# Moving a bias load on ScalarE's queue and a row copy on SyncE's queue in a fused attention and feed-forward kernel

## The chip, the cores and the metric

The kernel runs on one core of a Trainium2 chip. The metric is the device time of one execution in microseconds (us). A core has five engines that run their own instruction streams: TensorE (PE, matrix products; its weight loads are shown as PEld), VectorE (DVE), ScalarE (ACT), GpSimd (POOL) and SyncE (SP), which here only issues transfers. ScalarE and GpSimd issue transfers too. SPq, ACTq and POOLq are the instruction queues of these engines, and each works in order. Transfers of all queues share 16 DMA engines.

## What is computed

x has 2048 rows of 640 values. Its normalised rows xn go through two branches that are added to x:

```python
xn = _layernorm(x, axis=-1)
return x + _A_ref(xn, A_wqkv, A_wo) + _B_ref(xn, B_w1, B_b1, B_w2, B_b2)

# A: 32 heads of 20 values; each row looks at 8 rows, 2 apart, itself the first
q, k, v = (xn @ wqkv)            # three 640-wide parts
logits = einsum("bhsd,bhswd->bhsw", q, kg) * scale
o = einsum("bhsw,bhswd->bhsd", softmax(masked logits), vg)
A = o @ wo
# B: 640 -> 1536 -> 640
B = gelu(xn @ w1 + b1) @ w2 + b2
```

The code above is the reference cut to its core; kg and vg are the keys and values gathered at the 8 rows.

## The kernel before

The 2048 rows are worked on in four chunks of 512 rows, and a chunk in four blocks of 128. A chunk's stages are: statistics of its rows, normalised rows xn, their transposition into xnT (640 values on partitions), the projections to q, k and v, the products q times shifted k on VectorE (piece `qk`, L436), their folding (`pa`, L471), the logits as a matmul with head_of (`lg`, L479), softmax, the weighted values, the output product with wo, and the first and second feed-forward products (`f1`, L595, with gelu on ScalarE, `ge`, L611, and `o`, L631 and L633).

The order of the work is written out by hand. Each small step is a named piece, and the list `ORDER` (L42) says in which order the pieces are emitted. Every engine then runs its own instructions in that order, and an instruction waits on semaphores for what it needs. So moving a name in `ORDER` moves its instructions in the stream of each engine that the piece uses, and nothing else. In a name such as `xn12` the first digit is the chunk and the second the block.

Before `ORDER` starts, the loads are issued (L136 to L149): on SyncE x's block 0, wq, wk, blocks 2 and 3 of chunk 0, wv, chunk 1's rows and w1; on ScalarE x's block 1 (L138) and the bias b1 (L139). b1 comes as 12 rows of 128 values into the tile `b1_rt`, whose 16 rows GpSimd has set to zero (L124). The piece `tb` (L459) transposes it on TensorE into a PSUM tile, and the piece `b1` (L462) copies that on VectorE to `b1T`, from where each gelu takes its bias. The first gelu is `ge0_0`. `ldx` loads chunks 2 and 3 of x, `ldo` loads wo and b2, and `ld2` loads w2, all on SyncE.

Chunk 0 is normalised on VectorE (L268), transposed on TensorE (`tp`, L283) and copied to xnT by VectorE and ScalarE (`tc`, L288). Its projections are made by halves of 256 rows: `hj` is a group of matmuls (L383), and `hc` is ScalarE's copy of the result (L398). The first digit of these names is 0, 1 or 2 for q, k and v, the second is the half, and the third a group of columns, where group 2 is one 128-wide tile and the others are two. `hj102`, `hj101` and `hj100` are thus the keys of the first half.

Chunk 1's rows are normalised on ScalarE (L266: `xn13`, `xn10`, `xn11`, `xn12` in this order) and transposed by transposing DMAs on SyncE (`tc13`, `tc10`, `tc11`, `tc12`, L295). Chunk 1's first projection is `pj101` (L339); it needs all four blocks. ScalarE also makes the row sums of chunk 2 in between (`su`, L224, and `sq`, L231).

The output is put together in device memory: `xp0`, `xp1` and `xp2` copy rows of x to the output (L304, on SyncE), later accumulating DMAs on GpSimd add b2 (`xb`, L308) and the product of each block (`od`, L644). `xp0` copies chunk 0's 512 rows, 640 KB.

The PSUM tiles of projections, logits, first feed-forward products and `tb` come from one pool of six buffers (psA).

Of the kernel before, what the change touches and what calls it, by code (L numbers as in the profile page):

```python
# [17 lines left out]
P = 128  # L18
DH = D // H
PAD = (W - 1) * DIL  # L20
KT, FT = D // P, F // P
# [19 lines left out]

ORDER = """  # L42
wb st00a sum1 wa pad01 st00 rs00 ldx rc00 xn00a tp00a xn00b tp00b tc00a ga neg1 sq1 rs01 rc01 tc00b gb2 mean1 xn01
tp01 gb3 gb4 tc01a gd tc01b ho ge gc1 st03a st03 rs03 gc0 hj102 rc03 hc102 tb b1 hj101 hc101 st02a st02 rs02 hj100
hc100 xn03 tp03 tc03 pk hj202 rc02 xn02 tp02 tc02 gc4 hj201 hc201 hj111 st11a st10a hc111 st12a hj012 hc012 st11 hc202
st13a st13 hj112 hc112 st10 st12 rs1 qk010 rc1 qk000 qk011 hj110 f10_0 ge0_0 hj212 xn13 qk001 xn10 tc13 xn11 hc212
pa010 hj011 hj010 hc010 f10_11 f10_2 hc110 hc011 qk031 qk021 ge0_11 f10_10 xp0 qk020 pa000 su23 f10_6 xn12 ge0_10
qk030 pa020 su21 tc10 tc11 su22 hj200 hc200 f10_3 ge0_3 pa030 pa011 f10_9 tc12 su20 ng2 sq21 ge0_9 pa021 pj101 pc101
ge0_2 sq23 pj111 pj102 pj114 pc114 xp2 pc102 pj110 pc110 pj104 pa001 ge0_6 pa031 lg0 pc111 cl0 ldo xb3 xb2 pc104 mask
m0 mx0 ex0 pj112 pj103 pc103 pj113 pc113 ss0 ri0 pad11 pj100 pc100 pc112 qk121 qk120 hj211 sq20 hc211 qk101 ld2 pj124  # L50
qk100 sq22 pc124 f10_4 rs2 f11_6 pj121 rc2 ge0_4 pa120 qk110 f11_2 f10_1 ge0_1 pa121 qk111 xn21 pj123 pc123 ge1_6
# [26 lines left out]
def kernel(  # L78
# [16 lines left out]
    nc = tc.nc  # L95
# [27 lines left out]
    b1_rt = consts.tile([MW, P], BF16, name="b1_rt")  # L123
# [6 lines left out]
    def load_x(b0, b1):  # L130
        nc.sync.dma_start(x_sb[:, b0:b1, :], x_nb[:, b0:b1, :])  # L131
# [4 lines left out]
    load_x(0, 1)  # L136
    nc.vector.memset(x_sb[:, 1, 0:16], 0.0)
    nc.scalar.dma_start(x_sb[:, 1, :], x_nb[:, 1, :])  # L138
    nc.scalar.dma_start(b1_rt[0:FT, :], B_b1.rearrange("(t p) -> t p", p=P))  # L139
    for a in range(1):  # L140
        ks = slice(a * KT // 1, (a + 1) * KT // 1)
        nc.sync.dma_start(wqkv[0][:, ks, :], wqkv_v[:, ks, 0:D])
# [8 lines left out]

    def do_ldx():
        load_x(2 * BPC, NCH * BPC)

    def do_ld2():
        w2_v = B_w2.rearrange("(t p) n -> p t n", p=P)
        for c in range(2):
            ts = slice(c * FT // 2, (c + 1) * FT // 2)
            nc.sync.dma_start(w2_sb[:, ts, :], w2_v[:, ts, :])
# [20 lines left out]
    mask = consts.tile([H, W, MW], BF16, name="mask")  # L180
# [489 lines left out]
    def piece(name, fn, *args):  # L670
        assert name not in pieces
        pieces[name] = lambda: fn(*args)

    for name in "tb b1 mean1 ho ldx ld2 ldo xl oclo ohi ochi ochd mask pk".split():
        piece(name, locals()[f"do_{name}"])
    for u, a, b, eng, own in (("a", 0, 2, "ve", "lo"), ("b", 2, KT, "se", "hi")):
        piece(f"xn00{u}", do_xn, 0, 0, a, b)
# [119 lines left out]
```

## Time and profile before

| | |
|---|---|
| median of 3 runs | 207.31 us (206.66 to 207.37) |
| the profiled execution's own time | 207.25 us |
| its span, first to last instruction | 205.3 us |
| mean granted TensorE clock | 1.000 |
| packets moved by DMA | 27335, 31.77 MB, mean 155 GB/s |

The span is what the trace covers; the profiled execution's own time is 1.95 us longer. All times of single instructions are counted from the span's start. A row of the timeline gives start, duration, engine, line of the kernel, operation, output and input with shapes, the number of instructions merged into the row, and in brackets how long the engine stood idle before it and what ended that. A row of a list of DMA issues ends with the size and the median time from issue to landing. Busy times by stretch give for each engine the busy time and, in brackets, the number of instructions, then the granted clock, the DMA engines' mean busy share and the rate in GB/s.

### The profile page before, as it was taken

The page shows a single profiled execution, that of the slowest core. Times are in us where ns is not written, and L with a number is a line of the kernel's source. Part 1 is how long each engine was busy: PE and PEld are TensorE (multiplying, and loading weights), DVE is VectorE, ACT ScalarE, POOL GpSimd, SP SyncE. Part 2 cuts the span into 40 slices and gives each one's busy share as a digit, 9 for nine tenths or more (in the row PEclk, how much of TensorE's full clock was granted, in tenths as well). Part 3 has the DMA queues.
Part 4 walks back from the last instruction along what each step waited for, and adds up shares of the span by engine and source line. Part 5 has one row for each costly group of instructions (what it writes and reads, how often), then busy time and mean ns, then how long its engine had stood idle before and what let it go on. Part 6 is the DMA issues. An engine that isn't in the chain of part 4 may idle for free.

```text
span 205.3 us, 3230 instructions
## 1 busy us (share of the span) xinstructions
PE 200.1 (97%) x1261; PEld 111.1 (54%) x1261; DVE 181.6 (88%) x226; ACT 127.1 (62%) x246; POOL 34.6 (17%) x49
## 2 busy tenths in 40 slices
PE   8899999999999999999999999999999999999994
PEld 3798655464454555554555555445544455555552
DVE  3489999389998999769999999899998999699992
ACT  6388998999966998856425735564535794111210
POOL 2000000440000242202260060003104223111120
PEclk9999999999999999999999999999999999999999
DMA  6999599899259299989999067005462997972253
GB/s 209 390 395 374 185 140 323 303 258 199 58 100 252 86 173 190 156 128 182 189 188 191 8 73 122 0 0 68 103 134 32 164 190 118 209 116 28 28 66 64
DMA packets 27335, 31.77 MB, mean 155 GB/s; under 512 B 9272, under 2 KB 22072, under 8 KB 27320
## 3 DMA queue, kind: packets, MB, share of 16 engines
q0 software_dynamic: 7408, 12.78, 39.0%
q1 hardware_dynamic: 19600, 18.58, 32.8%
q8 instruction: 10, 0.16, 0.3%
q10 hardware_dynamic: 312, 0.20, 0.3%
q14 instruction: 5, 0.04, 0.1%
HBM read 10.00 MB, written 7.54 MB: 85 GB/s over the span
## 4 chain that ended last, share of the span: by engine, by line
PE 90%; DMA 4%; ACT 3%; issue 1%; SPq 0%; DVE 0%
PE lo L631 29%; PE pps L339 24%; PE hps L595 22%; PE hi L633 7%; PE gps L383 5%; DMA wq_sb<-in_A_wqkv_dram 3%; DMA xnT<-xn 2%; ACT xn L266 2%; PE gps L352 1%; PE L L479 1%; ACT qT L398 1%; PE tp L283 0%; ACT trash L224 0%; ACT hT L611 0%; SPq L131 0%
## 5 line engine op out<-in xcount | busy, mean ns | idle before, releaser
L595 PE MATMUL hps<-xnT,w_sb 128*128 128x512 bf16 x240 | 55.6, 379 | 0.0
L436 DVE TENSOR_TENSOR half<-qT,kT 128x2560 bf16<-128x2560 bf16 x32 | 46.7, 1484 | 1.0 <-PE L L479 0.9
L631 PE MATMUL lo<-w_sb,hT 128*128 128x512 bf16 x144 | 41.3, 379 | 0.0
L595 PEld LDWEIGHTS <-w_sb 128*128 128x128 bf16 x240 | 23.1, 98 | 26.2
L471 DVE TENSOR_TENSOR half<-half 128x1024 bf16<-128x1024 bf16 (+1 forms) x44 | 36.5, 881 | 0.0
L638 ACT CAST osb<-lo 128x512 bf16<-128x512 f32 x15 | 8.8, 584 | 37.1 <-PE hi L633 18.3
L633 PE MATMUL hi<-w_sb,hT 128*128 128x128 bf16 x144 | 31.5, 219 | 0.0
L611 ACT ACTIVATE hT<-hps,b1T 128x512 bf16<-128x512 f32 x36 | 24.0, 692 | 6.5 <-PE hps L595 5.6
L563 DVE TENSOR_TENSOR half<-vT,x_sb 128x2560 bf16<-128x2560 bf16 x16 | 23.0, 1487 | 3.3 <-DMA x_sb<-e 3.2
L644 POOL DMA_DIRECT2D out_dram<-osb x15 | 13.7, 959 | 72.2 <-ACT osb L639 72.2
L573 POOL DMA_DIRECT2D half<-half x12 | 15.6, 1302 | 56.0 <-DVE half L563 56.0
L563 DVE TENSOR_TENSOR half<-vT,ax 128x2560 bf16<-128x2560 bf16 x16 | 23.0, 1482 | 1.2 <-PE L L479 1.2
L631 PEld LDWEIGHTS <-hT 128*128 128x128 bf16 x144 | 14.1, 98 | 17.2 <-issue 0.4
L631 PE MATMUL lo<-wo,oT 128*128 128x512 bf16 x80 | 23.1, 379 | 0.0
L339 PE MATMUL pps<-xnT,wq_sb 128*128 128x512 bf16 x75 | 18.5, 380 | 0.4 <-DMA xnT<-xn 0.4
L339 PE MATMUL pps<-xnT,wv_sb 128*128 128x512 bf16 x75 | 18.3, 379 | 0.0
L339 PE MATMUL pps<-xnT,wk_sb 128*128 128x512 bf16 x75 | 18.0, 379 | 0.0
L633 PE MATMUL hi<-wo,oT 128*128 128x128 bf16 x80 | 16.9, 219 | 0.0
L176 ACT ACT_TABLE_LOAD x12 | 15.4, 1283 | 0.9 <-PEq L781 0.7
L633 PEld LDWEIGHTS <-hT 128*128 128x128 bf16 x144 | 14.1, 98 | 1.9
L582 DVE TENSOR_TENSOR half<-half 128x1280 bf16<-128x1280 bf16 x16 | 13.1, 821 | 0.5 <-DMA half<-half 0.4
L403 ACT CAST vT<-pps 128x512 bf16<-128x512 f32 x15 | 8.8, 587 | 6.9 <-PE pps L339 6.9
(91 smaller groups left out, 262.3 us busy)
## 6 DMA issues: line engine op xcount, KB each, us to landing
half<-half POOLq DMA_DIRECT2D x12, 640.0 KB, 6.9
w_sb<-in_B_w_dram SPq DMA_DIRECT2D x4, 960.0 KB, 11.3
out_dram<-osb POOLq DMA_DIRECT2D x15, 160.0 KB, 3.5
ax<-e SPq DMA_DIRECT2D x8, 256.0 KB, 4.7
x_sb<-e SPq DMA_DIRECT2D x8, 256.0 KB, 4.9
out_dram<-b2bc POOLq DMA_DIRECT2D x3, 640.0 KB, 9.6
x_sb<-in_A_x_dram SPq DMA_DIRECT2D x1, 1280.0 KB, 12.9
out_dram<-x_sb SPq DMA_DIRECT2D x2, 640.0 KB, 4.7
```

What stands on the lines that cost most here:

```text
L176: nc.scalar.activation(warm[:], nc.const_aps.tensor(0.0, [P, 1], F32), func)
L339: nc.tensor.matmul(ps[:], lhsT=wqkv_p[which][:, ti, to, :], rhs=xnT[:, ti, :], start=(ti == 0), stop=(ti == KT - 1),)
L436: nc.vector.tensor_tensor(out=half[:, j, h], in0=q[:, :, at].unsqueeze(1).to_broadcast([P, W // 2, KT, P]), in1=window(k, h, at), op=ALU.mult,
L471: nc.vector.tensor_tensor(out=kept, in0=kept, in1=gone, op=ALU.add)
L563: nc.vector.tensor_tensor(out=half[:, j, h], in0=window(qkv_tile(n, 2), h, cs), in1=ax_view(n)[:, j, ws, :].unsqueeze(2).to_broadcast([P, ...
L573: nc.gpsimd.dma_start(a, b, accum_op=ALU.add, max_dma_last_dim=CUT)
L582: nc.vector.tensor_tensor(out=a, in0=a, in1=b, op=ALU.add)
L595: nc.tensor.matmul(ps[:], lhsT=w1_sb[:, ti, ft * P : (ft + 1) * P], rhs=tiles["xnT", n][:, ti, :], start=(ti == 0), stop=(ti == KT - 1),)
L611: nc.scalar.activation(hT, tiles["hps", n, ft][:], ACT.Gelu_apprx_tanh, bias=b1T[:, ft : ft + 1], scale=1.0)
L631: nc.tensor.matmul(lo[:], lhsT=lhs, rhs=rhs[:, 0:CH], start=first, stop=last)
L633: nc.tensor.matmul(hi[:, 0 : D - CH], lhsT=lhs, rhs=rhs[:, CH:D], start=first, stop=last)
L644: nc.gpsimd.dma_start(rows, tiles["osb", n, bl][:], accum_op=ALU.add)
```

## The change

Two pieces of work change their place.

The load of b1 leaves the head of the kernel, where it stood second in ScalarE's queue, and becomes a piece of its own, `ldb`, between `hc102` and `hj101`. The pieces `tb` and `b1`, which stood there, go behind `st12`, the last of chunk 1's statistics, ahead of `rs1` and `qk010`.

The piece `xp0` leaves its place between `tc13` and `tc10` in SyncE's queue and goes behind `tc12`, ahead of `xp2`.

```diff
-hc102 tb b1 hj101 ... hj112 hc112 st10 st12 rs1 qk010
+hc102 ldb hj101 ... hj112 hc112 st10 st12 tb b1 rs1 qk010

-f10_10 xp0 qk020 ... tc10 tc11 ... tc12 su20
+f10_10 qk020 ... tc10 tc11 ... tc12 xp0 su20

     nc.scalar.dma_start(x_sb[:, 1, :], x_nb[:, 1, :])
-    nc.scalar.dma_start(b1_rt[0:FT, :], B_b1.rearrange("(t p) -> t p", p=P))

+    def do_ldb():
+        nc.scalar.dma_start(b1_rt[0:FT, :], B_b1.rearrange("(t p) -> t p", p=P))

-    for name in "tb b1 mean1 ho ldx ld2 ldo ...
+    for name in "tb b1 mean1 ho ldx ldb ld2 ldo ...
```

The first two parts are lines of `ORDER`, cut to the names around the moved ones. No instruction is added or taken away.

More of the change, by code (lines that the diff above doesn't have):

```diff
@@ L43 @@
 wb st00a sum1 wa pad01 st00 rs00 ldx rc00 xn00a tp00a xn00b tp00b tc00a ga neg1 sq1 rs01 rc01 tc00b gb2 mean1 xn01
[L44 to L48, printed above, removed]
+tp01 gb3 gb4 tc01a gd tc01b ho ge gc1 st03a st03 rs03 gc0 hj102 rc03 hc102 ldb hj101 hc101 st02a st02 rs02 hj100 hc100
+xn03 tp03 tc03 pk hj202 rc02 xn02 tp02 tc02 gc4 hj201 hc201 hj111 st11a st10a hc111 st12a hj012 hc012 st11 hc202 st13a
+st13 hj112 hc112 st10 st12 tb b1 rs1 qk010 rc1 qk000 qk011 hj110 f10_0 ge0_0 hj212 xn13 qk001 xn10 tc13 xn11 hc212
+pa010 hj011 hj010 hc010 f10_11 f10_2 hc110 hc011 qk031 qk021 ge0_11 f10_10 qk020 pa000 su23 f10_6 xn12 ge0_10 qk030
+pa020 su21 tc10 tc11 su22 hj200 hc200 f10_3 ge0_3 pa030 pa011 f10_9 tc12 xp0 su20 ng2 sq21 ge0_9 pa021 pj101 pc101
 ge0_2 sq23 pj111 pj102 pj114 pc114 xp2 pc102 pj110 pc110 pj104 pa001 ge0_6 pa031 lg0 pc111 cl0 ldo xb3 xb2 pc104 mask
@@ L672, in piece @@
         pieces[name] = lambda: fn(*args)
-    for name in "tb b1 mean1 ho ldx ld2 ldo xl oclo ohi ochi ochd mask pk".split():
+    for name in "tb b1 mean1 ho ldx ldb ld2 ldo xl oclo ohi ochi ochd mask pk".split():
         piece(name, locals()[f"do_{name}"])
```

## The prediction

> **What bounds the kernel now.** I read the page's first parts and then one narrow view at a time. The page says which engine carries the end:
>
> ```profile
> span 205.3 us, 3230 instructions
> PE 200.1 (97%) x1261; PEld 111.1 (54%) x1261; DVE 181.6 (88%) x226; ACT 127.1 (62%) x246; POOL 34.6 (17%) x49
> ```
>
> TensorE (PE) is busy for 200.1 of 205.3 us. An edit can therefore pay only by filling one of PE's few gaps, or cost by making a new one. The busy time by stretch shows where the gaps are (behind the stretch: its length, then PE's busy time; the granted clock is the figure before the last two):
>
> ```profile
> 6.77:29.85 23.08, 23.08 (x206) 18.47 (x206) 20.00 (x37) 19.03 (x40) 0.00 (x0) 1.00 0.95 291
> 29.85:30.28 0.43, 0.00 (x1) 0.03 (x1) 0.43 (x2) 0.43 (x2) 0.00 (x0) 1.00 0.44 167
> 30.28:202.00 171.72, 171.72 (x1028) 90.33 (x1029) 157.65 (x178) 103.45 (x197) 33.26 (x32) 1.00 0.70 134
> ```
>
> From the first weights' arrival at 6.77 until 202 us PE has one gap, 0.43 us long, before 30.28. The clock is 1.00 throughout, so no throttling enters the sum. The chain that ended last, in order of time (start, duration), says what that gap waits for:
>
> ```profile
> 25.73 0.81 ACT xn L266
> 26.56 3.58 DMA xnT<-xn
> 30.28 6.64 PE pps L339 x30
> ```
>
> Chunk 1's first projection needs all four transposed blocks. ScalarE (ACT) finishes the last one, xn12, at 26.54 (25.73 + 0.81); its transposing DMA is issued at 26.56 and has landed 3.58 us later, at 30.14. PE's only inner gap hangs on the very DMAs that the second edit reorders.
>
> **Second edit: the copy xp0 goes behind the transposes.** SyncE's queue (SPq) around them, from the timeline, then the landing times of the transposes issued at 23.11, 24.88 and 26.56:
>
> ```profile
> 21.12 1.32 SPq L295 DMA_TRANSPOSE xnT<-xn  x1
> 22.55 0.50 SPq L304 DMA_DIRECT2D out_dram<-x_sb  x1
> 23.11 1.68 SPq L295 DMA_TRANSPOSE xnT<-xn  x1
> 24.88 1.23 SPq L295 DMA_TRANSPOSE xnT<-xn  x1
> 26.56 2.34 SPq L295 DMA_TRANSPOSE xnT<-xn  x1
> 28.99 0.53 SPq L304 DMA_DIRECT2D out_dram<-x_sb  x1
> ...
> xnT<-xn SPq DMA_TRANSPOSE x1, 5.8
> xnT<-xn SPq DMA_TRANSPOSE x1, 4.6
> xnT<-xn SPq DMA_TRANSPOSE x1, 3.6
> ```
>
> Chunk 2's four transposes follow each other with no copy between them; they are the undisturbed case (first the four issues, then their median time to landing):
>
> ```profile
> 53.65 5.23 SPq L295 DMA_TRANSPOSE xnT<-xn  x4
> xnT<-xn SPq DMA_TRANSPOSE x4, 2.4
> ```
>
> There a transpose lands in 2.4 us. Behind xp0 they take 5.8, 4.6 and 3.6, and the last issue stretches to 2.34 us: the 640 KB copy stands ahead in the same queue, and the backlog drains one transpose at a time. With xp0 out of its place the second can be issued at about 22.55 and the third at 23.9 (an issue of 1.3 later), so both are down by 26.3 (23.9 + 2.4). The last still starts at 26.56, since ACT sets that, and after 2.4 us lands at 28.96. PE arrives at 29.85, so the DMA is 0.9 us early and the gap goes: **-0.43 us**. More isn't there, since PE is busy on both sides of it. The condition is a landing below 3.29 us (29.85 - 26.56).
>
> What is late next? The first matmul behind the gap that needs VectorE (DVE) is lg0, and the last DVE group before it is this:
>
> ```profile
> 31.21 4.76 DVE L471 TENSOR_TENSOR half<-half 128x2048 bf16<-128x2048 bf16 x6
> 36.86 1.05 PE L479 MATMUL L<-half,head_of 128*32 128x512 bf16 x16
> ```
>
> DVE ends at 35.97; PE will ask at 36.43 instead of 36.86, so 0.46 us of cover is left. Past lg0, DVE's softmax starts from ACT's copy of lg0's result and moves with it. On SPq the last transpose's issue falls from 2.34 to about 1.23, xp0's 0.50 follows, and the next copy goes out at about 28.4 instead of 28.99. But xp0's bytes now stand ahead of it and of the loads of wo, b2 and w2. Their users:
>
> ```profile
> 31.37 1.79 SPq L159 DMA_DIRECT2D w_sb<-in_B_w_dram  x2
> 38.91 4.07 POOL L308 DMA_DIRECT2D out_dram<-b2bc  x3 [36.96 <-DMA b2bc<-in_B_b_dram]
> 54.23 0.22 PE lo L631
> ```
>
> The copy's own landing time bounds the lateness by some 3.5 us. w2, issued by 33.16 and 11.3 us on its way by the median of the page's w loads, is there at 44.5; its first user runs at 54.23, so 9.7 us cover it. b2's user is an accumulating DMA on GpSimd (POOL), which is idle for 36.96 us before it and busy for 17% of the span. I cost both at nothing.
>
> **First edit: b1's load goes behind hc102, its transpose tb and DVE's copy behind st12.** What goes at the start (ACTq is ACT's instruction queue):
>
> ```profile
> 0.73 1.28 ACT L176 ACT_TABLE_LOAD   x1 [0.73 <-PEq L781]
> 1.33 0.65 ACTq L139 DMA_DIRECT2D b_rt<-in_B_b_dram  x1
> 2.03 0.20 ACT L176 ACTIVATE warm<-const-float32-0.0 128x1 f32<-128x1 f32 x1
> ```
>
> The issue (until 1.98) lies wholly beside the table load (until 2.01), so its removal gains nothing. The same rows show that ACT issues a DMA while an earlier instruction still executes. Where it goes:
>
> ```profile
> 11.46 0.37 ACT L398 CAST kT<-gps 128x256 bf16<-128x256 f32 x1
> 11.95 0.58 ACT L398 CAST kT<-gps 128x512 bf16<-128x512 f32 x1
> 12.43 0.30 ACT L248 ACTIVATE std<-mv,eps_t 128x1 f32<-128x1 f32 x1
> 13.04 0.58 ACT L398 CAST kT<-gps 128x512 bf16<-128x512 f32 x1 [0.31 <-PE gps L383]
> ```
>
> Issued beside hc102 at 11.46, 0.65 us ends at 12.11, and hc101 starts 0.16 late. Issued after hc102's end at 11.83, it ends at 12.48 and hc101 is 0.53 late. Queued behind it are hc101, rs02, hc100 and the copies of blocks 3 and 2. ACT has 0.31 us of idle time ahead of hc100, so at that point the delay is between nothing and 0.22 us; I take nothing, as the start's row shows the overlap. One row speaks for far more: with its queue full, SPq needed 1.88 us for one issue:
>
> ```profile
> 9.01 1.88 SPq L131 DMA_DIRECT2D x_sb<-in_A_x_dram  x1
> ```
>
> That upper end is a rival below. [...]
>
> tb and the copy of b1 change places:
>
> ```profile
> 10.52 0.18 PE L459 MATMUL tb<-ident,b_rt 16*128 16x16 bf16 x1
> 11.21 0.15 DVE L462 CAST b1T<-tb 128x12 f32<-128x12 bf16 x1
> 16.68 1.80 PE L383 MATMUL gps<-xnT,wk_sb 128*128 128x256 bf16 x15
> 17.43 1.44 DVE L436 TENSOR_TENSOR half<-qT,kT 128x2560 bf16<-128x2560 bf16 x1
> ```
>
> PE loses 0.18 at 10.52 and gets it back behind the first five of the fifteen matmuls, at about 17.3: zero. DVE saves 0.15 early and pays 0.15, with up to 0.2 of waiting for tb, ahead of 17.43. DVE has no idle time from there to lg0, so lg0's inputs come up to 0.35 us later: within the 0.46 above, hence nothing; without that cover at most 0.35.
>
> The new wait is tb's, for b1. b1's last packets were still moving some 3.5 us after its issue at 1.33 (queue q10 in the stretch 4.75 to 5.25), while SPq's queue q1 was full:
>
> ```profile
> q1 hardware_dynamic: 156, 0.19, 105.2%
> q10 hardware_dynamic: 2, 0.00, 0.3%
> ```
>
> Issued by 12.11, such a load is down by about 16 (12.11 + 3.9), 1.3 us ahead of tb. [...]
>
> **Sum.** 207.25 (the profiled execution: the span of 205.3 and 1.95 around it) - 0.43 = **206.8 us**. The median of the three runs, 207.31, is 0.06 above that execution.
>
> **Rivals.**
> 1. *No gain.* The last transpose still needs over 3.29 us, because its delay came from its neighbours and not from xp0. For it: its landing of 3.6 is the shortest of the three and xp0 is the farthest away by then. Against: the undisturbed 2.4, with the same spacing. Time: 207.25.
> 2. *The issue on ACT takes 1.88 us*, as SPq's did. hc101 then starts at 13.34 and hc100 at 14.12 instead of 13.04 (0.48 and 0.30 for the two before it); about 1.1 us pass through xn02 and the copies to PE, and 0.43 comes back: 207.9. Against: only SPq's own full queue shows such issues.
> 3. *Slower: b1 stands behind q1's backlog.* This stretch shows the backlog's end (last two figures: DMA share, GB/s):
>
> ```profile
> 20.00:21.00 1.00, 1.00 (x11) 1.00 (x10) 1.00 (x2) 1.00 (x3) 0.00 (x0) 1.00 0.32 115
> ```
>
> At a share of 0.32 the queue runs dry at about 20.3. tb, asked at 17.3, holds PE for 3.0 us, and everything behind it: 207.25 + 3.0 - 0.43 = 209.8. It decides from a landing of b1 after 17.3, over 5 us from issue; the q10 row speaks against it.
>
> **How the numbers follow.** The forecast 0.56, rival 1 0.22, rival 2 0.12, rival 3 0.08; 0.02 for a gain that I don't see. Half a per cent, about what a measurement of this kernel can tell from no change, is 1.04 us: the forecast, rival 1 and most of rival 2 lie within it. Slower by more: rival 3 and the worst of rival 2, 0.11. Faster by more: 0.05, the forecast with the scatter of the runs shown (206.66 to 207.37) on its side. The range reaches from 206.3 (the forecast less that scatter) to 208.0 (rival 2); rival 3 stays out.
>
> **What would show it.** Right: PE busy without a gap before chunk 1's first projection, the last transpose landing in about 2.4 us, its issue near 1.2; no idle time of PE ahead of tb; ACT's issue of b1 at most 0.65. Wrong: a landing above 3.29; PE waiting at tb or at lg0; the first 128x512 kT copy starting after 12.5.

## The result, and the profile after

| | before | after |
|---|---|---|
| median of 21 runs each, taken together | 206.92 us (206.28 to 207.37) | 206.28 us (205.77 to 207.35) |
| the profiled execution's own time | 207.25 us | 206.68 us |
| its span | 205.3 us | 204.9 us |

The ratio of after to before is 0.9975, with a 95% interval of 0.9964 to 0.9986: 0.5 us less, between 0.3 and 0.75. The forecast's 0.43 us (a ratio of 0.9979) lies inside. The change is smaller than the half per cent that the prediction took as about what a measurement of this kernel can tell from no change.

The page of the changed kernel begins thus:

```profile
span 204.9 us, 3232 instructions
PE 201.0 (98%) x1261; PEld 111.8 (55%) x1261; DVE 181.6 (89%) x226; ACT 127.2 (62%) x246; POOL 34.6 (17%) x49
```

Each engine has as many instructions as before (the two more of the first line are semaphore instructions), and the gain is in PE's gaps. All lines of the changed kernel after the loads stand two lines lower than before. The same view by stretches, with its borders at the new times of the same matmuls:

```profile
6.44:29.48 23.04, 23.04 (x207) 18.66 (x207) 20.57 (x40) 19.39 (x41) 0.00 (x0) 1.00 0.84 282
29.48:190.00 160.52, 160.52 (x949) 84.12 (x947) 147.66 (x167) 101.63 (x191) 30.67 (x29) 1.00 0.74 143
190.00:202.50 12.50, 11.84 (x87) 6.38 (x85) 11.07 (x14) 2.26 (x6) 2.58 (x3) 1.00 0.35 41
```

PE's busy time equals the stretch in the first two rows: from the first weights' arrival to 190 us it stands still nowhere, and the gap of 0.43 before chunk 1's first projection is gone. SyncE's queue there, from the timeline:

```profile
20.74 1.31 SPq L297 DMA_TRANSPOSE xnT<-xn  x1
22.16 1.21 SPq L297 DMA_TRANSPOSE xnT<-xn  x1
23.46 1.23 SPq L297 DMA_TRANSPOSE xnT<-xn  x1
26.19 1.24 SPq L297 DMA_TRANSPOSE xnT<-xn  x1
27.53 1.07 SPq L306 DMA_DIRECT2D out_dram<-x_sb  x2
```

And the median landing time of the four transposes, then those of xp0, of the last transpose and of the third (issued at 23.46):

```profile
xnT<-xn SPq DMA_TRANSPOSE x4, 2.5
...
out_dram<-x_sb SPq DMA_DIRECT2D x1, 640.0 KB, 3.3
xnT<-xn SPq DMA_TRANSPOSE x1, 2.4
...
xnT<-xn SPq DMA_TRANSPOSE x1, 4.6
```

The last transpose is issued at 26.19 and is down at 28.6, 0.7 us before PE asks. The median hides that the third one still takes 4.6 us, as long as in the kernel before, though no copy stands ahead of it. It is down at 28.1 (23.46 + 4.6), where the prediction had it down by 26.3; that is still 1.2 us ahead of PE. What stands around the old gap, in the timeline:

```profile
29.32 1.24 PE L341 MATMUL pps<-xnT,wq_sb 128*128 128x512 bf16 x5
30.84 4.76 DVE L473 TENSOR_TENSOR half<-half 128x2048 bf16<-128x2048 bf16 x6
35.89 1.05 PE L481 MATMUL L<-half,head_of 128*32 128x512 bf16 x16
```

The first row carries no bracket, so PE waited for nothing. DVE ends at 35.60 (30.84 + 4.76), and lg0 starts at 35.89 without a wait: 0.29 us of the cover is left.

The bias edit, from the timeline of ACT and its queue, of PE with its weight loads, and of DVE:

```profile
10.26 0.57 ACTq L155 DMA_DIRECT2D b_rt<-in_B_b_dram  x1
10.33 0.57 ACT L378 CAST qT<-gps 128x512 bf16<-128x512 f32 x1
10.79 0.38 ACT L400 CAST kT<-gps 128x256 bf16<-128x256 f32 x1
11.34 0.58 ACT L400 CAST kT<-gps 128x512 bf16<-128x512 f32 x1 [0.17 <-PE gps L385]
12.43 0.58 ACT L400 CAST kT<-gps 128x512 bf16<-128x512 f32 x1 [0.31 <-PE gps L385]
...
16.71 0.18 PE L461 MATMUL tb<-ident,b_rt 16*128 16x16 bf16 x1
...
16.92 0.17 DVE L464 CAST b1T<-tb 128x12 f32<-128x12 bf16 x1
```

The DMA is issued at 10.26 while the two instructions ahead of it, gc0 and hc102, are still to run; hc101 and hc100 then wait for PE and not for the issue, so it costs nothing. tb doesn't wait for b1. The packets of ACT's queue q10 in the stretch 13.75 to 14.25, beside SPq's full queue q1, show when b1 moved:

```profile
q1 hardware_dynamic: 122, 0.19, 103.2%
q10 hardware_dynamic: 24, 0.00, 4.0%
```

That is 3.5 to 4 us after the issue, about as in the kernel before, and 2.5 us ahead of tb.

**Stage by stage.** The starts of three instructions in the two profiled executions, and in those of four runs told of below (us):

| | first wq matmul | chunk 1's first projection | lg0 |
|---|---|---|---|
| before | 6.77 | 30.28 (23.51 later) | 36.86 |
| after | 6.44 | 29.32 (22.88 later) | 35.89 |
| changed kernel once more | 6.44 | 29.32 (22.88) | 35.89 |
| bias edit alone | 6.25 | 29.74 (23.49) | 36.32 |
| copy edit alone | 6.44 | 29.48 (23.04) | 36.04 |
| copy edit alone, once more | 7.13 | 30.04 (22.91) | 36.61 |

At lg0 the changed kernel is 0.97 ahead: 0.33 because the first weights came earlier, and 0.63 from the stage with the gap. That is 0.20 more than the 0.43 that the trace calls idle. A matmul of 512 columns has a row of 0.379 us in the profile of the kernel before, while 30 of them in a line take 6.64 (its chain), so the next starts 0.216 behind it ((6.64 - 0.379) / 29); by an estimate from these rows the gap cost its idle time and the 0.163 by which the last matmul's row outlasts that spacing. The remaining 0.04 is not accounted for.

Of the 0.97 the profiled execution kept only 0.4 at the end of its span. In its tail an accumulating DMA within SBUF, issued by POOL for chunk 2's weighted values, is waited for by DVE:

```profile
172.41 1.20 POOL L575 DMA_DIRECT2D half<-half  x1 [2.40 <-DVE half L565]
...
183.08 0.82 DVE L584 TENSOR_TENSOR half<-half 128x1280 bf16<-128x1280 bf16 x1 [0.94 <-DMA half<-half]
```

Whether that is a new wait that eats part of the gain or an accident of one execution was put to a test below.

### The profile page after: what moved, and what is told of

Its sections match the earlier page's. It is cut to its first block, busy times and chain, and to the rows that moved or that the text cites. A ratio compares the mean times of both kernels' runs of the same rounds, so it can differ in the third digit from the quotient of the medians.

```text
span 204.9 us, 3232 instructions
## 1 busy us (share of the span) xinstructions
PE 201.0 (98%) x1261; PEld 111.8 (55%) x1261; DVE 181.6 (89%) x226; ACT 127.2 (62%) x246; POOL 34.6 (17%) x49
## 4 chain that ended last, share of the span: by engine, by line
PE 76%; DVE 12%; DMA 5%; issue 4%; POOL 1%; ACT 1%; POOLq 0%; DVEq 0%
PE pps L341 23%; PE hps L597 22%; PE lo L633 15%; PE gps L385 7%; DVE half L565 5%; DMA half<-half 5%; PE hi L635 4%; PE idle L451 2%; DVE half L577 2%; DVE half L584 2%; PE gps L354 1%; PE L L481 1%; DVE oT L588 1%; POOL half L575 1%; PE tp L285 1%
## 5 line engine op out<-in xcount | busy, mean ns | idle before, releaser
L597 PEld LDWEIGHTS <-w_sb 128*128 128x128 bf16 x240 | 23.1, 98 | 26.2
L633 PEld LDWEIGHTS <-oT 128*128 128x128 bf16 x80 | 7.7, 98 | 10.2 <-DVE oT L588 1.3
```

The source lines that it names most:

```text
L597: nc.tensor.matmul(ps[:], lhsT=w1_sb[:, ti, ft * P : (ft + 1) * P], rhs=tiles["xnT", n][:, ti, :], start=(ti == 0), stop=(ti == KT - 1),)
L633: nc.tensor.matmul(lo[:], lhsT=lhs, rhs=rhs[:, 0:CH], start=first, stop=last)
```

## The experiments

The theory: the whole gain comes from xp0 leaving its place ahead of the transposes, and the bias edit is free. Rivals: the bias edit carries part of the gain, by an emptier start or by DVE's order, or it costs something; the landing depends on the number of the transposes' neighbours and not on the copy's bytes; a wait at the tail takes part of the gain back.

**The bias edit alone.** The changed kernel with xp0 in its old place:

```diff
-f10_10 qk020 ... tc12 xp0 su20
+f10_10 xp0 qk020 ... tc12 su20
```

> Only the first edit: b1's load, tb and the copy of b1 move, xp0 stays between tc13 and tc10. Theory (the gain is the gap before chunk 1's first projection, the bias costs nothing): the gap of about 0.4 us stays, the last transpose still lands after more than 3.3 us, the time is that of before within 0.2 us. Rival (b1's load at the head slows the first weights): wq lands earlier than 5.5 us after its issue, PE's first projection starts before 6.7, and the time falls by 0.2 to 0.4 us though the gap stays.

Measured: 206.92 us beside 206.81, ratio 1.0026 (1.0000 to 1.0052). PE and SPq in its timeline:

```profile
26.10 2.25 SPq L297 DMA_TRANSPOSE xnT<-xn  x1
...
29.74 1.25 PE L341 MATMUL pps<-xnT,wq_sb 128*128 128x512 bf16 x5 [0.35 <-DMA xnT<-xn]
```

The gap and the long issue are back with xp0. The early start of the first matmul (6.25) is there too, and brought nothing at the end. Run a second time in the last comparison:

> The first edit alone once more. Theory: the time of before within 0.1%. Rival: 0.1 to 0.3% above before, as in the first reading (1.0026, 1.0000 to 1.0052).

206.81 beside 206.85, ratio 0.9986 (0.9965 to 1.0008), with the gap again:

```profile
30.32 1.25 PE L341 MATMUL pps<-xnT,wq_sb 128*128 128x512 bf16 x5 [0.56 <-DMA xnT<-xn]
```

The bias edit makes no difference that these runs can tell.

**The copy edit alone.** The kernel before with one name moved:

```diff
-f10_10 xp0 qk020 ... tc12 su20
+f10_10 qk020 ... tc12 xp0 su20
```

> Only the second edit: xp0 goes behind tc12. Theory: the last transpose lands after 2.4 to 2.6 us, its issue takes about 1.2, PE has no gap before chunk 1's first projection, and the time falls by 0.4 us (0.2%). Rival (the gain comes from the bias load): the time stays that of before.

Measured: 206.14 beside 206.81, ratio 0.9962 (0.9943 to 0.9981). From its timeline the last transpose's issue, then the landing time of the four:

```profile
26.35 1.21 SPq L295 DMA_TRANSPOSE xnT<-xn  x1
```

```profile
xnT<-xn SPq DMA_TRANSPOSE x4, 2.4
```

The gain and its cause are here in full. The four transposes are as many as before, so it isn't their number that delays the last one. Twice more, each time beside the changed kernel itself on the same chip:

> The second edit alone again, for the comparison with the changed kernel on the same chip. Theory: 0.2 to 0.4% below before and equal to the changed kernel within 0.1%. Rival: 0.2 to 0.6 us below the changed kernel.

> The changed kernel again, beside the copy-only kernel on the same chip. Theory (the bias edit costs nothing): the same time as the copy-only kernel within 0.1%, both 0.2 to 0.4% below before. Rival (the bias edit costs 0.1 to 0.3%, as the difference of the first readings suggests): 0.2 to 0.6 us above the copy-only kernel.

Copy edit alone 205.96, ratio 0.9976 (0.9964 to 0.9989); changed kernel 206.12, ratio 0.9992 (0.9968 to 1.0015); before 206.66. The second interval holds no change as well as a gain of 0.3%; it didn't settle the size, so both ran again:

> The second edit alone once more. Theory: 0.2 to 0.4% below before, equal to the changed kernel within 0.1%.

> The changed kernel once more, beside each edit alone on the same chip. Theory (the bias edit costs nothing, the copy edit brings 0.43 us): equal to the copy-only kernel within 0.1%, 0.2 to 0.3% below before. Rival (the bias edit costs 0.1 to 0.3%): above the copy-only kernel by that much.

Copy edit alone 205.92, ratio 0.9953 (0.9929 to 0.9978); changed kernel 206.04, ratio 0.9953 (0.9930 to 0.9975); before 206.85. The two are equal within the intervals, with the medians of the copy edit alone lower by 0.16 and 0.12. So the copy edit carries the whole gain. As both differences have the same sign, a cost of some 0.1 us for the bias edit isn't excluded.

In the first of these profiles of the copy edit alone the first matmul came late:

```profile
7.13 1.03 PE L352 MATMUL gps<-xnT,wq_sb 128*128 128x128 bf16 x15 [0.75 <-DMA wq_sb<-in_A_wqkv_dram]
```

Over the profiled executions with b1's load at the head this start lies between 6.06 and 7.64 (six of them), with the load moved between 6.24 and 6.53 (eight). The load's place may narrow that scatter; the medians above show no gain from it, and it stays open.

**The copy ahead of the last transpose only.** The kernel before with xp0 behind the third:

```diff
-f10_10 xp0 qk020 ... tc10 tc11 su22 ... tc12 su20
+f10_10 qk020 ... tc10 tc11 xp0 su22 ... tc12 su20
```

> The kernel before with xp0 between the third and the last transpose instead of behind the first. Theory by bytes (a transpose waits only until the copy's 640 KB are through): xp0 is issued at about 25.2, its bytes are through by about 28, the last transpose lands at 28.9 to 29.5, so PE has no gap and the time is that of the copy-only kernel. Rival (a transpose right behind a copy drains slowly beyond the copy's own bytes, as the one issued at 23.11 took 5.8 us though the copy had landed at 26.1): the last transpose lands 4.5 to 6 us after its issue at 26.2, PE's gap is 0.9 to 2.7 us, and the time is 0.5 to 2.3 us above before's.

Measured: 206.61 beside 206.66, ratio 1.0003 (0.9979 to 1.0027). From its timeline:

```profile
24.44 0.53 SPq L304 DMA_DIRECT2D out_dram<-x_sb  x1
25.85 1.44 SPq L295 DMA_TRANSPOSE xnT<-xn  x1
...
29.32 0.38 PE L339 MATMUL pps<-xnT,wq_sb 128*128 128x512 bf16 x1 [0.18 <-DMA xnT<-xn]
```

The last transpose, issued 1.4 us behind xp0, takes 3.3 us to land and is down at 29.15, as the theory had it, but just too late: a gap of 0.18. The time expected, that of the copy edit alone, was missed: the median is that of the kernel before, and the profiled execution (206.05) is the fastest of the twelve, so its small gap may not be the usual one.

The landing doesn't go by the copy's bytes alone. Here the copy has landed at 28.5 (24.44 + 4.1), and the transpose behind it 0.6 us later. In the kernel before, the copy had landed at 26.1 (22.55 + 3.5) and the transpose issued behind it only at 28.9; from 27.15 to 28.45 the DMA engines moved 10 GB/s. And without a copy ahead of it the third transpose takes 4.6 us in the changed kernel's profile and 4.0 here. So something besides the copy holds the transposes up at this point; with xp0 ahead, the last one may be held up by it too. The traces of the kernel before and of the changed one have three packets of the instruction queues (one of 16 KB on q8, two of 8 KB on q14) between 24.6 and 26.2, and none while chunk 2's transposes move, whose median landing time is 2.4 in both. That fits, but whether these packets are the cause was not tested.

**Both copies ahead.** The kernel before with xp2 (1,120 KB) put right behind xp0, so that 1,760 KB instead of 640 stand ahead:

```diff
-f10_10 xp0 qk020 ... pc114 xp2 pc102
+f10_10 xp0 xp2 qk020 ... pc114 pc102
```

> The kernel before with the copy xp2 (1120 KB) moved next to xp0, so that 1760 KB instead of 640 KB stand ahead of the last three transposes. Theory (the transposes wait for the copies' bytes): about 2.8 us of bytes more at 400 GB/s, the last transpose lands between 30.7 and 32.0 on the trace's clock, PE's gap grows to 0.9 to 2.2 us, the time rises by 0.4 to 1.8 us. Rival (the transposes delay one another, the copy doesn't matter): the gap stays near 0.4 us and the time that of before.

Measured: 211.91 beside 206.81, ratio 1.0218 (1.0183 to 1.0253), some 4.5 us: the direction was right, the size missed by far. The profiled execution took 214.5 us, the longest of the six, so its sizes are an upper end. SPq and PE in its timeline:

```profile
24.57 5.09 SPq L295 DMA_TRANSPOSE xnT<-xn  x2
...
29.75 1.29 SPq L295 DMA_TRANSPOSE xnT<-xn  x1
...
34.41 2.33 PE L339 MATMUL pps<-xnT,wq_sb 128*128 128x512 bf16 x5 [3.69 <-DMA xnT<-xn]
```

Two things had been left out. With both copies ahead, the issues of the next two transposes took 5.09 us, so the last one was issued at 29.75, 2.3 us after ACT had finished its input at 27.4. And five matmuls take 2.33 instead of 1.25. The stretches show the granted clock beside it (the figure before the last two):

```profile
31.00:32.00 1.00, 0.00 (x0) 0.00 (x0) 1.00 (x1) 0.94 (x4) 0.00 (x0) 1.00 2.47 111
32.50:33.00 0.50, 0.00 (x0) 0.00 (x0) 0.50 (x1) 0.50 (x2) 0.00 (x0) 0.97 0.59 53
33.00:34.00 1.00, 0.00 (x0) 0.00 (x0) 1.00 (x2) 0.10 (x1) 0.00 (x0) 0.50 1.24 320
38.00:39.00 1.00, 1.00 (x4) 0.30 (x2) 0.00 (x0) 0.75 (x2) 0.43 (x1) 0.50 1.02 357
39.00:40.00 1.00, 1.00 (x4) 0.42 (x3) 0.00 (x0) 0.00 (x0) 1.00 (x2) 0.60 1.05 390
```

While PE waits, its clock falls to 0.50; a mean of 0.97 in the second row puts the fall at 32.97, one of 0.60 in the last the return at 39.8. From 34.41 to 39.8 PE works at that clock and, as an estimate, loses half of these 5.39 us, 2.7. With 3.3 from the gap (3.69 less 0.43), 0.9 from a first matmul that came later (7.64 instead of 6.77) and 0.3 from one more wait at 110 us, that is 7.2 us, by which this execution's span is longer (212.5 against 205.3). Not every execution has the slower clock: the mean granted clocks of the six are 0.984 (214.5 and 212.65 us), 0.992 (211.99, 211.84 and 210.87) and 1.000 (210.21). The one at 1.000 is 3.4 us above the kernel before, about the gap's 3.69 less the 0.43 that was there; the five with a lower clock took 0.66 to 4.3 us longer than that one.

**b1 asked for too early.** Rival 3's wait, brought about: the changed kernel with tb and b1 right behind hc100:

```diff
-hc100 xn03 ... st12 tb b1 rs1
+hc100 tb b1 xn03 ... st12 rs1
```

> The changed kernel with tb and the copy of b1 right behind hc100 instead of behind st12, so that PE asks for b1 at about 12.4 us, 2.1 us after its load is issued. Theory (the load's packets wait their turn in the full DMA engines; in the changed kernel they moved at 13.75 to 14.25): PE stands idle ahead of tb for about 2 us, until 14.3 to 14.8, and the time rises by about 2 us above the changed kernel's. Rival (such a load lands after 2.6 us as x's block 1 does at the head): idle for about 0.5 us, and the time rises by 0.5 us.

Measured: 210.94 beside 206.66, ratio 1.0215 (1.0186 to 1.0244), 4.8 us above the changed kernel in the same comparison (206.12). From PE's timeline:

```profile
14.24 0.18 PE L461 MATMUL tb<-ident,b_rt 16*128 16x16 bf16 x1 [1.99 <-DMA b_rt<-in_B_b_dram]
15.04 0.71 PE L285 MATMUL tp<-ident,xn 128*128 128x128 bf16 x5 [0.62 <-DVE xn L270]
```

The wait is what b1's landing at 14.2 gives, 2.0 us, and 0.62 for DVE, whose b1 had stood waiting ahead of xn03. The granted clock is low behind it again:

```profile
13.00:14.00 1.00, 0.00 (x0) 0.00 (x0) 0.00 (x0) 0.00 (x0) 0.00 (x0) 1.00 1.04 379
14.50:15.00 0.50, 0.00 (x0) 0.00 (x0) 0.50 (x3) 0.00 (x0) 0.00 (x0) 0.93 1.07 402
15.00:16.00 1.00, 0.96 (x8) 0.84 (x9) 0.96 (x4) 0.21 (x1) 0.00 (x0) 0.50 1.06 399
17.00:18.00 1.00, 1.00 (x8) 0.74 (x6) 0.97 (x4) 0.61 (x2) 0.00 (x0) 0.50 1.05 392
18.00:18.50 0.50, 0.50 (x4) 0.40 (x3) 0.47 (x3) 0.35 (x2) 0.00 (x0) 0.66 1.07 398
18.50:19.00 0.50, 0.50 (x7) 0.50 (x6) 0.47 (x3) 0.00 (x0) 0.00 (x0) 1.00 1.07 399
```

From 14.93 to 18.34 the clock is 0.50; PE, busy from 15.04, loses by the same estimate half of 3.3, some 1.65 us. With 2.61 of waiting that is 4.3 us, which from 206.1 gives 210.4; the profiled execution took 210.28. The median of the six lies 0.66 above that execution, and no trace shows what the longer ones wait for.

**b1 asked for a little later.** The same with tb behind tp02, and DVE's copy left at its place, so that the wait is shorter:

```diff
-tp02 tc02 ... st12 tb b1 rs1
+tp02 tb tc02 ... st12 b1 rs1
```

> The changed kernel with tb on PE behind tp02, where PE asks for b1 at about 13.3 us; the copy of b1 on VectorE stays behind st12. b1 landed at 14.2 in the kernel that asked at 12.25. Theory: PE stands idle for about 0.9 us. If the granted clock falls only behind a gap of two microseconds or more, it stays at 1.00 here and the time rises by 0.9 us above the changed kernel's. Rival (any gap of a microsecond brings the low clock): the clock falls to 0.50 for some 3 us and the time rises by more than 2 us.

Measured: 207.32 beside 206.85, ratio 1.0017 (0.9989 to 1.0045), 1.3 us above the changed kernel in the same comparison (206.04). The wait, then the stretch behind it:

```profile
15.10 0.18 PE L461 MATMUL tb<-ident,b_rt 16*128 16x16 bf16 x1 [1.40 <-DMA b_rt<-in_B_b_dram]
```

```profile
16.00:18.00 2.00, 2.00 (x21) 2.00 (x20) 1.93 (x7) 0.96 (x2) 0.00 (x0) 1.00 1.06 396
```

The wait was expected at 0.9 us; b1 landed at 15.1 and not at 14.2. A wait of 1.40 us costs 1.3 us, and the clock stays at 1.00: the lowest mean clock of the twelve executions is 0.999.

**The tail's wait.** The changed kernel with the last part of chunk 2's accumulation taken from the DMA and done by DVE, a little later:

```diff
-BY_DMA = ((0, 1, 2, 3), (0, 1, 2, 3), (0, 1, 2, 3), ())
+BY_DMA = ((0, 1, 2, 3), (0, 1, 2, 3), (0, 1, 3), ())

-av221 aa22 pj320 ... ot20 ge3_9
+av221 pj320 ... ot20 aa22 ge3_9
```

> The changed kernel, with the addition aa22 of chunk 2 made by VectorE instead of by an accumulating DMA and placed behind ot20. Theory (the lead is partly lost because VectorE waits 0.94 us for that DMA at 183 us and sets the end from there): the wait goes, the addition of 1.49 us fills VectorE's idle time at 173 us, and the time falls by 0.3 to 0.9 us below the changed kernel's. Rival (VectorE has no room, or the end hangs on something else): the time is that of the changed kernel or up to 1 us above it.

Measured: 206.18 beside 206.81, ratio 0.9968 (0.9944 to 0.9992). In its profile the wait is gone, and lg0 to PE's end takes 165.61 us instead of 166.23; yet the median is the changed kernel's. The second profile of the changed kernel has no such loss either (span 204.3, own time 206.07). The wait belongs to single executions and isn't what the change's time consists of. No version tried was measurably faster than the changed kernel or the copy edit alone.

## Why the prediction was right, point by point

- **The gap goes because xp0 leaves.** Right, and shown: it is there in every profile with xp0 ahead of the transposes, gone in every one with xp0 behind them, and 0.18 long with xp0 in between. The last transpose lands in 2.4 us as the undisturbed ones did (2.4 in the profiles of the changed kernel and of the copy edit alone; in a repetition of each the median of the four is 2.5 and 2.6), and its issue is 1.24 (expected: near 1.23). That the copy's bytes alone make it late is not shown: the third transpose takes 4.6 us with and without them. The prediction had the second and third down by 26.3; the third is down at 28.1, and only the 1.2 us left ahead of PE kept that error without a price.
- **-0.43 us.** The sign and the mechanism held, the size was a little low: 0.47 to 0.63 in the profiles from the first matmul to the projection, 0.5 (0.3 to 0.75) between the medians. The term left out is, by the estimate above, the 0.163 us of the last matmul's row beyond the spacing of matmuls. With it the sum would have been 207.25 - 0.59 = 206.7.
- **The forecast of 206.8** stands beside a median of 206.28, and 206.68 for the profiled execution. Of the 0.54 us between 206.82 and the median, 0.33 is the kernel before itself: the sum starts from 207.25, and its 21 runs have a median of 206.92. The other 0.21 is the gain, 0.64 between the medians instead of 0.43. The lower bound, 206.3, is just missed by that median. It doesn't follow from its own words either: the forecast less the scatter of 206.66 to 207.37 is 206.1 (206.82 - 0.71), and with that the median lies inside. The time by the ratio, 207.31 x 0.9975 = 206.8, is the forecast's.
- **"What is late next".** DVE kept its cover at lg0: 0.29 us left, of the 0.46 less the 0.35 at most that had been allowed for. xp0 behind the transposes delayed nothing that shows in the first two profiles of the changed kernel: PE has no gap until 190 us. A third one has a wait of 0.32 us for a later chunk's transposes at 102.5 us; its cause stays open.
- **ACT's issue at nothing.** Right: 0.57 us, issued ahead of its neighbours' turn; hc101 and hc100 wait for PE. Rival 2 (1.88 us) didn't occur. The first full-sized key copy starts at 11.34, before the 12.5 that would have spoken against it.
- **b1's landing.** The lag of 3.9 us held, but the issue went out at 10.26 instead of by 12.11, so b1 was down at 14.2 and not at 16; the margin was 2.5 instead of 1.3 us. Rival 3 failed on the q10 row, as argued.
- **Rival 3's price** was the mis-sized one. Its 3.0 us of waiting were put down at 3.0; waits of 2.0 and 0.62 us cost 4.8, with the clock at 0.50 for some 3.4 us. With half of these 3.4 us on top, that rival would have stood near 211.5 (209.8 + 1.7, an estimate) instead of 209.8. "The clock is 1.00 throughout, so no throttling enters the sum" was true of the forecast, but a rival with 3.0 us of waiting couldn't rest on it: with waits of 1.99 and 0.62 us the clock fell to 0.50, with one of 1.40 us it stayed at 1.00.

## What to carry to other kernels

Where one engine is busy for 97% of the span, look for its few gaps and go back from each to the transfer that ended last; if that shares a queue with a bulk copy whose result nobody waits for, put the copy behind it; here a gap of 0.43 us gave 0.47 to 0.63 in the profiles. Weigh a new wait on the matmul engine by its length: here 1.4 us cost 1.3, while 2.0 and 0.6 us, with 0.2 between them, cost 4.8. Before trusting half a per cent, run the parts alone and more than once: the first repetition of the changed kernel alone would have left its gain open.

## What the runs showed of the hardware

- The granted clock fell to 0.50 after waits of 1.99 and 0.62 us for some 3.4 us (14.93 to 18.34), and during one of 3.69 us for some 6.8 us (32.97 to 39.8); at a wait of 1.40 us it stayed at 1.00. These times are worked out from the mean clocks of the stretches above. Up to the fall PE had stood idle for 1.99 and then 0.51 us, with tb's 0.18 between them, in the one case and for 2.25 us (from 30.72) in the other. With both copies ahead the mean granted clock was 0.984 in two of six executions, 0.992 in three and 1.000 in one; as an estimate, 0.50 for 3.4 of some 210 us makes a mean of 0.992 and for 6.8 us one of 0.984. What brings the fall about and what sets its length isn't shown by these runs.
- With a plain copy ahead in the same queue transposing DMAs landed later. The next one behind 640 KB took 5.8 us in the kernel before, instead of 2.4, and the last of the four 3.6 there and 3.5 with the bias edit alone, instead of 2.4 (3.3 with the copy 1.4 us ahead of it). The third took 4.6 with the copy ahead, and 4.6 and 4.0 without, so the copy isn't the only thing that delays them. With 1,760 KB ahead two issues together took 5.09 us, where two without a copy ahead took 2.4 (1.21 and 1.23 above).
- A load of 12 rows of 256 bytes on ACT's queue moved 3.5 to 4 us after its issue at 10.26 in the changed kernel, while q1, SyncE's queue, stood at 103.2%; where PE waited for this load, the wait ended at 14.24 and at 15.10. ACT's instructions ran on beside the issue: it lasted from 10.26 to 10.83, and two casts started at 10.33 and 10.79.
